# Fused attention and MLP on one core: q and k of batch 2 turned by DMA transposes instead of TensorE

## The chip, the cores and the metric

The kernel runs on one core of a Trainium2 chip. Its engines are TensorE (PE in the profile; PEld is its weight load), VectorE (DVE), ScalarE (ACT), GpSimd (POOL) and SyncE (SP). Each works through its own instructions in order and they wait for each other by semaphores. Sixteen DMA engines move data; here POOL issues the loads, and SP the DMA transposes, the small row copies and the stores of the output. POOL's loads go into one queue (q0 in the profile), SP's into another (q1). The metric is the device time of one execution in microseconds (us), the median over several.

## The reference

Attention with a forgetting decay over 8 batches, 8 heads, 576 tokens, head dimension 64, then a two-layer MLP with the activation h - tanh(h) on all 4,608 tokens:

```python
scores = scale * np.matmul(q, k.transpose(0, 1, 3, 2))
log_f = np.log(np.clip(f, 0.0001, 1.0))
cum = np.cumsum(log_f, axis=-1)
decay = cum[:, :, :, None] - cum[:, :, None, :]
scores = np.where(causal, -1000000000.0, scores + decay)
attn = softmax(scores)                     # written out, with 1e-09 in the divisor
x = (attn @ v).transpose(0, 2, 1, 3).reshape(B * S, H * D)
h = x @ w_in                               # 512 -> 2048
out = (h - np.tanh(h)) @ w_out             # 2048 -> 512
```

## The kernel before

**Slots and pairs.** Attention is done for pairs of heads: 8 batches of 4 pairs, 32 in all. The main loop (L595) runs over slots p = 0 to 32. Slot p emits the scores of pair p in seven tiles (`TILES`, L278; each tile has its matmuls L315, an exp on ACT L324, and from batch 1 on a mask on POOL L334), the values of pair p-1 (matmuls L346, normalised on DVE L353 to L355 into `xn`), and the turn of that pair's output into `XR`, the MLP's input (`turn`, L358: from batch 1 on two DMA transposes on SP, L369 and L371). `att_items` (L537) lists these in order, tile by tile; batch 2 is slots 8 to 11, and slots from 4 on are not "early".

**The MLP in between.** The MLP works on nine units of 512 tokens. A first-layer step (`mlp1`, L387) is four matmuls into one PSUM bank (L397), a tanh on ACT (L402) and a sum on DVE into `gq` (L406). Unit 0's second layer is plain (L432, 16 steps of four matmuls; four steps make one output tile, and the third and fourth of them read the second half of `wout`). Units 1 to 8 use a seven-product scheme with sums and differences of blocks (steps L456; sums of `gq` on DVE, L424, S3 being the first; differences of weights `W1`, `W2`, `W4` and a block of `wout`, L234). `TAKE` says how many MLP steps each slot takes; the loop at L610 spreads them over the slot's items. The banks for the first layer come from a ring (L374): three banks at first, and four, with `ps_tr` added, once `widen(1)` is called in slot 11.

**q and k.** The scores need q and k with the head dimension on the partitions (`QT`, `KT`, two buffers each, by batch parity). There are two ways.
- Batches 0 to 2 (`FAR = 3`): `load_qk` (L89) loads 96 partitions with rows of 768 bytes; in the slot before a pair is used `trans` (L243) turns it on PE (six transposes for q, six for k, L253, into a bank of `ps_tr`), and two copies take it to `QT` or `KT`: for q the first on DVE (L266), the second on ACT (L264) in slots from 4 on, for k both on DVE. k's transposes use the same bank as q's, so they wait for q's second copy.
- Batches 3 to 7: `load_block` (L94) loads five blocks of up to 128 tokens with rows of 128 bytes; `turn_block` (L99) turns each by a DMA transpose on SP (L101) into `TQ` or `TK` (one buffer each); `place` (L103) copies from there into `QT` and `KT`, four copies each, on ACT (L106), DVE or POOL (L108).

**What is emitted where.** `LOADS` maps (slot, tile) to loads, transposes, places and weight differences, and `att_items` emits them there, behind the scores of that tile. Around the change: the halves of `wout` at (4, 0) and (4, 2), q and k of batch 2 at (4, 5) and (4, 6), its v blocks at (5, 0) to (5, 4), the first weight difference at (7, 1). Order on an engine is the order of emission; what is behind a waiting instruction on its engine waits too. POOL's loads share eight semaphores in turn, so that a load is issued only when the eighth load before it has landed.

Of the kernel before, what the change touches and what calls it, by code (L numbers as in the profile page):

```python
# [8 lines left out]
FP32 = mybir.dt.float32  # L9
# [5 lines left out]
PITCH = 640  # L15
VW = 66
SHIFT = 5.0
FAR = 3


@with_exitstack
def kernel(
# [11 lines left out]
    P = 128  # L34
# [48 lines left out]
    vn = [qkp.tile([P, NJ, H, VW], FP16, tag=f"vn{i}", name=f"vn{i}") for i in range(2)]  # L83
    QT = [qkp.tile([D + 3, H, S], FP16, tag=f"QT{i}", name=f"QT{i}") for i in range(2)]
    KT = [qkp.tile([D + 3, H, PITCH], FP16, tag=f"KT{i}", name=f"KT{i}") for i in range(2)]
    TQ = qkp.tile([P, NPAIR, S], FP16, tag="TQ", name="TQ")
    TK = qkp.tile([P, NPAIR, S], FP16, tag="TK", name="TK")

    def load_qk(dst, src, b, h0, h1):  # L89
# [29 lines left out]
        nc.gpsimd.dma_start(out=vn[b % 2][:, n, h0:h1, 0:D],  # L119
                            in_=v[b, h0:h1, n * P:(n + 1) * P, :].rearrange("h p d -> p h d"))  # L120

    lf = TQ[0:NH, :, :].rearrange("p c s -> p (c s)").bitcast(FP32)[:, 0:S]
# [35 lines left out]
    cum = TQ[0:NH, :, :].rearrange("p c s -> p (c s)").bitcast(FP32)[:, S:2 * S]  # L158
# [33 lines left out]
    def load_wout(t0, t1):  # L192
# [7 lines left out]
             (1, 5): [lambda: load_v_rest(1), lambda: load_v_head(1, 0)],  # L200
             (2, 1): [lambda: load_v_head(1, 1), lambda: load_win(DFF // 2, DFF)],
             (4, 0): [lambda: load_wout(0, NFT // 2)],
             (4, 2): [lambda: load_wout(NFT // 2, NFT)]}
    for n in range(NJ - 1):
        LOADS.setdefault((3, n), []).append(lambda n=n: load_v_block(1, n, 2, H))
    LOADS.setdefault((NPAIR, 5), []).append(lambda: load_qk(qn, q, 2, 0, H))
    LOADS.setdefault((NPAIR, 6), []).append(lambda: load_qk(kn, k, 2, 0, H))
    for b in range(2, B):
        p0 = (b - 1) * NPAIR
        for n in range(NJ - 1):  # L210
            LOADS.setdefault((p0 + 1, n), []).append(lambda b=b, n=n: load_v_block(b, n, 0, H))
        LOADS.setdefault((p0 + 1, 4), []).append(lambda b=b: load_v_rest(b))
        LOADS.setdefault((p0, 0), []).append(lambda b=b: load_aug(b))
        if b < FAR:
            continue
        for n in range(NJ):
            qs, ts = ((p0 - 1, n), (p0, 4)) if b == FAR else ((p0 - 2, n + 2), (p0 - 1, 3 if b == FAR + 1 else 1))
            LOADS.setdefault(qs, []).append(lambda b=b, n=n: load_block(qb, q, b, n))
            LOADS.setdefault((p0, n), []).append(lambda b=b, n=n: load_block(kb, k, b, n))
            LOADS.setdefault(ts, []).append(lambda b=b, n=n: turn_block(TQ, qb, b, n))  # L220
            LOADS.setdefault((p0 + 1, 4), []).append(lambda b=b, n=n: turn_block(TK, kb, b, n))
        parts = [(dst, src, a, c) for dst, src in ((QT, TQ), (KT, TK)) for a in range(2) for c in (0, 2)]
        spots = [(p0, 3, "A"), (p0, 5, "A"), (p0 + 1, 0, "A"), (p0 + 1, 2, "A")] + [(p0 + 3, ti, "V") for ti in range(4)]
        if b == FAR:
            spots = [(p0 + 3, ti, eng) for ti, eng in zip((0, 1, 2, 0, 1, 2, 4, 5), "AVAPPPPP")]
        elif b == FAR + 1:
            spots[0:4] = (p0, 5, "A"), (p0, 6, "A"), (p0 + 1, 0, "A"), (p0 + 1, 2, "V")
        for (slot, ti, eng), (dst, src, a, c) in zip(spots, parts):
            LOADS.setdefault((slot, ti), []).append(lambda b=b, dst=dst, src=src, a=a, c=c, eng=eng: place(
                dst, src, b, a, c, eng))  # L230

    def weights(o, x, y, n):
        ks = slice(n * NK // 2, (n + 1) * NK // 2)
        nc.vector.tensor_tensor(out=o[:, ks, :], in0=x[:, ks, :], in1=y[:, ks, :], op=ALU.subtract)  # L234

    SPOTS = [(7, 1), (7, 2), (7, 4), (7, 5), (8, 1), (8, 2), (10, 6), (11, 0)]
    for i, (o, x, y) in enumerate(((W1, B12, B11), (W2, B22, W1), (W4, B21, W2), (B12, B22, B12))):
        for n in range(2):
            LOADS.setdefault(SPOTS[2 * i + n], []).append(lambda o=o, x=x, y=y, n=n: weights(o, x, y, n))
# [3 lines left out]
    def trans(b, c, src, dst, early, copies, split=False):  # L243
        pn, g3 = S // NT6, NT6 // 2
        if early:
            t32 = ps_m.tile([P, UW], FP32, tag="m", name="t32")
            t16 = t32.bitcast(FP16)[:, 0:2 * S // 2].rearrange("p (a g n) -> p a g n", a=2, g=g3)
        else:
            t32 = ps_tr.tile([P, UW], FP32, tag="tr", name="t32")
            t16 = t32.bitcast(FP16)[:, 0:2 * S // 2].rearrange("p (a g n) -> p a g n", a=2, g=g3)  # L250
        for a in range(2):
            for g in range(g3):
                nc.tensor.transpose(out=t16[:, a, g, :],  # L253
                                    in_=src[b % 2][:, 2 * c + a, 2 * g:2 * g + 2, :],
                                    identity=id16[0:pn, 0:pn])
        parts = [(a, e) for a in range(2) for e in range(2)] if split else [(slice(0, 2), e) for e in range(2)]

        def copy(a, e, eng):
            if split:
                a = slice(a, a + 1)  # L260
            to = dst[b % 2][0:D, 2 * c:2 * c + 2, e:S:2].rearrange("d a (p g) -> d a p g", g=g3)[:, a]
            of = t16[e * D:(e + 1) * D, :, :, :].rearrange("d a g p -> d a p g")[:, a]
            if eng == "A":
                nc.scalar.activation(out=to, in_=of, func=AF.Copy)  # L264
            else:
                nc.vector.tensor_copy(out=to, in_=of)  # L266

        todo = [lambda a=a, e=e, eng=eng: copy(a, e, eng) for (a, e), eng in zip(parts, copies)]
        for fn in todo[:2]:
            fn()  # L270
        return todo[2:]

    def head_tiles(a):
        return [[(a, 0, 0, 512, 0)],
                [(a, 1, P, 448, 0), (a, 0, 512, 64, 448)],
                [(a, 2, 2 * P, 320, 0), (a, 3, 3 * P, 192, 320)]]

    TILES = head_tiles(0) + [[(0, 4, 512, 64, 64), (1, 4, 512, 64, 128)]] + head_tiles(1)  # L278
    LAST = 3
# [107 lines left out]
    def mlp1(u, ft, part=None):  # L387
        if part != 1:
            HP[(u, ft)] = bank("hps")
        hps = HP[(u, ft)]  # L390
        t0 = u * UW % RING
        parts = [(0, t0, min(UW, RING - t0))]
        if t0 + UW > RING:
            parts.append((RING - t0, 0, t0 + UW - RING))
        for o, t, n in parts:
            for ci in {None: range(NCH), 0: range(NCH - 1), 1: (NCH - 1,)}[part]:
                nc.tensor.matmul(out=hps[:, o:o + n], lhsT=win[:, ci, ft * P:(ft + 1) * P],  # L397
                                 rhs=XR[:, ci, t:t + n], start=(ci == 0), stop=(ci == NCH - 1))
# [7 lines left out]
        nc.vector.tensor_tensor(out=GQ[(u, i)][:, half, kt, :], in0=hps, in1=th, op=ALU.add)  # L406
        if u >= PLAIN:
            at = (12, 13, 14, 15) if u == 1 else (3, 6, 9, 12)
            if ft in at:
                sums(u, "S3", at.index(ft))  # L410

# [99 lines left out]
    def start():  # L511
        unread(33)
        q_rest = trans(*pairs[0], qn, QT, True, "AAAA", True)
        nc.scalar.activation(out=cq, in_=cum, func=AF.Copy, bias=-SHIFT * inv_qscale, scale=inv_qscale)
        nc.scalar.activation(out=expo, in_=lf[0:1, 0:1], func=AF.Exp)
        unread(6)
        k_rest = trans(*pairs[0], kn, KT, True, "VVVV", True)
        unread(22)
# [18 lines left out]
    def att_items(p):  # L537
# [5 lines left out]
        before = pairs[p - 1] if 0 < p <= len(pairs) else None  # L543
        after = pairs[p + 1] if p + 1 < len(pairs) else None
        early = p < NPAIR
        for ti in range(len(TILES)):
            if here and (p > 0 or ti > 1):
                put(scores, *here, ti)
# [4 lines left out]
                put(unread, 2)  # L553
            if p == 1 and ti == 3:
                put(last)
            for load in LOADS.get((p, ti), ()):
                items.append((load, False))
            at_q, at_k = (1, 3) if p == 0 else (0, 1) if early else (0, 2) if p == NPAIR else (0, 2)
            if ti == at_q and after and after[0] < FAR:
                put(trans, *after, qn, QT, early, "VV" if early else "VA")  # L560
            if p == NPAIR:
                if ti in (3, 4):
                    put(mlp1, 0, ti - 3, 1)
# [84 lines left out]
```

## Time and profile before

| what | us |
|---|---|
| median of 3 runs | 352.4 (352.31 to 352.46) |
| the profiled execution, whole | 352.82 |
| its span in the profile | 351.0 |
| PE busy | 336.5 (96%) |
| DVE, ACT, POOL busy | 259.9, 236.0, 167.6 |
| PE transposes of q and k, L253 (x144) | 10.3 |
| first-layer matmuls, L397 (x640) | 141.4 |

The whole execution is 1.8 us longer than the span of the profile. A matmul's row in the profile ends later than the next one can begin, so time lost on PE is read from start to start. The timeline's column in brackets is the idle time before a group and what ended it. Some rows that matter for the copies (line, engine, operation, out<-in, count; busy us, mean ns of one):

```profile
L266 DVE COPY KT<-t 64x576 f16<-64x576 f16 x22 | 17.6, 800 | 3.8 <-PE t L253 3.6
L106 ACT ACTIVATE QT<-TQ 64x1152 f16<-64x1152 f16 x17 | 19.7, 1158 | 0.2
L264 ACT ACTIVATE QT<-t 64x576 f16<-64x576 f16 x7 | 5.7, 812 | 8.2 <-DVE QT L266 8.2
L108 DVE COPY KT<-TK 64x1152 f16<-64x1152 f16 x16 | 7.4, 460 | 0.2
L108 POOL COPY KT<-TK 64x1152 f16<-64x1152 f16 x4 | 5.3, 1323 | 0.1
```

### The profile page before, as it was taken

The numbers are of one execution on the slowest core, as the hardware profiler recorded it, in microseconds if no ns is written. First come the engines' busy times: TensorE is split into PE (matmuls) and PEld (weight loads), VectorE is DVE, ScalarE is ACT, GpSimd is POOL, SyncE is SP. The second block draws the span as 40 slices with busy tenths as digits, with TensorE's granted clock in tenths as the row PEclk, the third lists the DMA queues.
The fourth block names the chain that finished last, engine by engine and source line by source line (L and its number), as shares of the span: only waits on it lengthen the run. The fifth ranks groups of instructions, "written<-read, shape, count | busy, mean of one in ns | idle before, by whom it ended". The sixth has DMA issues, their size and how long they took to land.

```text
span 351.0 us, 8590 instructions
## 1 busy us (share of the span) xinstructions
PE 336.5 (96%) x3253; PEld 230.7 (66%) x3253; DVE 259.9 (74%) x493; ACT 236.0 (67%) x433; POOL 167.6 (48%) x324
## 2 busy tenths in 40 slices
PE   8998888999889999999999999999999999999996
PEld 7476444555458655875588888855885587477485
DVE  7597577747799588767876787678767866876874
ACT  5587777668695778588868886888648841742640
POOL 8873563776499656575657564752322210000000
PEclk9999999999999999999999999999999999999999
DMA  9999999999978999699969996992031013003003
GB/s 112 144 166 202 192 206 127 112 150 175 113 62 110 152 169 133 77 172 159 114 78 179 151 111 88 174 157 42 23 102 49 18 36 122 0 2 120 0 6 115
DMA packets 144876, 38.79 MB, mean 111 GB/s; under 512 B 128148, under 2 KB 143236, under 8 KB 144836
## 3 DMA queue, kind: packets, MB, share of 16 engines
q0 software_dynamic: 92480, 18.39, 69.7%
q1 hardware_dynamic: 52356, 19.88, 29.7%
q8 instruction: 25, 0.41, 0.5%
q14 instruction: 15, 0.12, 0.1%
HBM read 36.85 MB, written 9.44 MB: 132 GB/s over the span
## 4 chain that ended last, share of the span: by engine, by line
PE 77%; DVE 11%; ACT 7%; issue 2%; DMA 1%; POOL 1%; ACTq 0%; DVEq 0%; POOLq 0%
PE hps L397 28%; PE ops L456 26%; PE ps L315 10%; PE av L346 6%; PE ops L432 3%; ACT e L324 3%; DVE KT L266 3%; DVE gq L406 2%; ACT th L402 2%; DVE QT L266 2%; DVE xn L355 1%; ACT QT L264 1%; PE t L253 1%; DVE gq L424 1%; DMA TQ<-in_f_dram 1%
## 5 line engine op out<-in xcount | busy, mean ns | idle before, releaser
L397 PE MATMUL hps<-XR,win 128*128 128x512 f16 (+1 forms) x640 | 141.4, 357 | 3.1 <-DVE gq L406 1.6
L406 DVE TENSOR_TENSOR gq<-hps,th 128x512 f16<-128x512 f32 x144 | 98.6, 687 | 33.1 <-ACT th L402 31.8
L324 ACT ACTIVATE e<-ps 128x512 f16<-128x512 f32 x192 | 110.0, 598 | 15.5 <-PE ps L315 7.9
L402 ACT ACTIVATE th<-hps 128x512 f32<-128x512 f32 x144 | 86.8, 604 | 49.5 <-PE hps L397 44.3
L334 POOL TENSOR_SCALAR_AFFINE_SELECT e<-e 128x128 f16<-128x128 f16 x168 | 60.6, 363 | 76.7 <-ACT e L324 74.8
L397 PEld LDWEIGHTS <-win 128*128 128x128 f16 x640 | 57.6, 97 | 50.3 <-issue 2.8
L315 PE MATMUL ps<-QT,KT 67*128 67x64 f16 (+5 forms) x384 | 77.2, 276 | 3.1 <-ACT e L324 2.4
L456 PEld LDWEIGHTS <-gq 128*128 128x128 f16 x640 | 60.3, 97 | 12.3 <-DVE gq L424 1.4
L456 PE MATMUL ops<-wout,gq 128*128 128x256 f16 x512 | 63.3, 272 | 1.1 <-DVE gq L424 1.1
L315 PEld LDWEIGHTS <-KT 67*128 67x128 f16 (+1 forms) x384 | 36.9, 98 | 27.9 <-issue 4.8
L346 PEld LDWEIGHTS <-e 128*128 128x128 f16 x896 | 32.1, 97 | 3.1
L346 PE MATMUL av<-vn,e 128*128 128x65 f16 x896 | 33.6, 193 | 0.0
L119 POOL DMA_DIRECT2D vn<-in_v_dram x32 | 28.0, 877 | 10.6 <-DMA win<-in_moe_w_in_dram 4.1
L456 PE MATMUL ops<-W,sq 128*128 128x256 f16 x256 | 31.2, 272 | 0.0
L355 DVE TENSOR_TENSOR xn<-av,rs 128x640 f16<-128x640 f32 x32 | 26.4, 825 | 1.1
L456 PEld LDWEIGHTS <-sq 128*128 128x128 f16 x256 | 24.2, 98 | 3.4
L266 DVE COPY KT<-t 64x576 f16<-64x576 f16 (+1 forms) x26 | 19.5, 750 | 3.8 <-PE t L253 3.6
L334 POOL TENSOR_SCALAR_AFFINE_SELECT el<-el 128x128 f16<-128x128 f16 x28 | 9.5, 338 | 26.8 <-ACT el L324 26.7
L96 POOL DMA_DIRECT2D qn<-in_q_dram x25 | 21.2, 846 | 0.7 <-issue 0.4
L96 POOL DMA_DIRECT2D kn<-in_k_dram x25 | 21.1, 846 | 0.6 <-issue 0.3
L106 ACT ACTIVATE QT<-TQ 64x1152 f16<-64x1152 f16 x17 | 19.7, 1158 | 0.2
L266 DVE COPY QT<-t 64x576 f16<-64x576 f16 x15 | 11.9, 795 | 7.6 <-PE t L253 7.6
(83 smaller groups left out, 301.9 us busy)
## 6 DMA issues: line engine op xcount, KB each, us to landing
out_dram<-ost SPq DMA_DIRECT2D x34, 256.0 KB
vn<-in_v_dram POOLq DMA_DIRECT2D x24, 128.0 KB, 5.6
qn<-in_q_dram POOLq DMA_DIRECT2D x20, 128.0 KB, 4.9
kn<-in_k_dram POOLq DMA_DIRECT2D x20, 128.0 KB, 4.5
win<-in_moe_w_in_dram POOLq DMA_DIRECT2D x2, 1024.0 KB, 14.8
wout<-in_moe_w_out_dram POOLq DMA_DIRECT2D x2, 1024.0 KB, 14.0
XR<-xn SPq DMA_TRANSPOSE x56
vn<-in_v_dram POOLq DMA_DIRECT2D x12, 64.0 KB, 4.8
```

The source lines that it names most:

```text
L96: nc.gpsimd.dma_start(out=dst[b % 2][0:pn, n, :].rearrange("p (h d) -> p h d", h=H), in_=src[b, :, n * P:n * P + pn, :].rearrange("h p d - ...
L119: nc.gpsimd.dma_start(out=vn[b % 2][:, n, h0:h1, 0:D], in_=v[b, h0:h1, n * P:(n + 1) * P, :].rearrange("h p d -> p h d"))
L266: nc.vector.tensor_copy(out=to, in_=of)
L315: nc.tensor.matmul(out=ps[:, col:col + n], lhsT=KT[b % 2][0:rows, h, j * P:(j + 1) * P], rhs=QT[b % 2][0:rows, h, i0:i0 + n], start=not ow ...
L324: nc.scalar.activation(out=e[:, lo:hi], in_=ps[:, lo:hi], func=AF.Exp, scale=qscale)
L334: nc.gpsimd.affine_select(out=view, in_=view, compare_op=ALU.is_ge, fill=0.0, base=0, pattern=pat, channel_multiplier=-1)
L346: nc.tensor.matmul(out=av[:, a, ib, :], lhsT=E.pop((b, c, a, j, ib)), rhs=vn[b % 2][:, j, 2 * c + a, 0:D + 1], start=(j == 0), stop=(j == ib))
L355: nc.vector.tensor_tensor(out=xn.rearrange("p i (a d) -> p a i d", a=2), in0=av[:, :, :, 0:D], in1=rs.to_broadcast([P, 2, NJ, D]), op=ALU. ...
L397: nc.tensor.matmul(out=hps[:, o:o + n], lhsT=win[:, ci, ft * P:(ft + 1) * P], rhs=XR[:, ci, t:t + n], start=(ci == 0), stop=(ci == NCH - 1))
L402: nc.scalar.activation(out=th, in_=hps, func=AF.Tanh, scale=-1.0)
L406: nc.vector.tensor_tensor(out=GQ[(u, i)][:, half, kt, :], in0=hps, in1=th, op=ALU.add)
L456: nc.tensor.matmul(out=ps[:, m, :], lhsT=LHS[lhs](u, kt // 4)[:, kt % 4, m * P:(m + 1) * P], rhs=rhs[:, kt, :], start=(fresh and (apart or ...
```

## The change

`FAR` becomes 2: batch 2 too is loaded in blocks, turned by DMA transposes and placed by copies. `TQ` gets a second buffer. A table by batch says where blocks are loaded, turned and placed; for batch 2 the q blocks are loaded at (4, 1) to (4, 5), the k blocks at (4, 6), (5, 0), (5, 2), (5, 3), (5, 4), the transposes are issued at (5, 1) for q and (6, 0) for k, and the copies stand in slots 7 and 8. The second half of `wout` moves from (4, 2) to (5, 1), behind the q blocks and two k blocks, and batch 2's v blocks from slot 5 to slot 6. All places of q are on ACT and all of k on DVE (batch 3's had been on ACT, DVE and POOL, batch 4's fourth on DVE).

For batch 1 in slots 4 to 6 `trans` now gives only the first copy at once; the second is given one tile later (`rest`), and q's second is on DVE. The ring of four banks starts with slot 7 in place of slot 11, when the last PE transpose is done. The S3 sums of unit 1 stand at steps 3, 6, 9, 12 like those of the other units, and the weight differences get other spots.

```diff
-FAR = 3
+FAR = 2
-    TQ = qkp.tile([P, NPAIR, S], FP16, tag="TQ", name="TQ")
+    TQ = [qkp.tile([P, NPAIR, S], FP16, tag=f"TQ{i}", name=f"TQ{i}") for i in range(2)]
...
-             (4, 2): [lambda: load_wout(NFT // 2, NFT)]}
+             (5, 1): [lambda: load_wout(NFT // 2, NFT)]}
...
-    LOADS.setdefault((NPAIR, 5), []).append(lambda: load_qk(qn, q, 2, 0, H))
-    LOADS.setdefault((NPAIR, 6), []).append(lambda: load_qk(kn, k, 2, 0, H))
+    def add(where, fn, *args):
+        LOADS.setdefault(where, []).append(lambda: fn(*args))
+
     for b in range(2, B):
         p0 = (b - 1) * NPAIR
...
-        if b < FAR:
-            continue
+        at_q = [(p0 - 2, n + 2) for n in range(NJ)]
+        at_k = [(p0, n) for n in range(NJ)]
+        at_v = [(p0 + 1, n) for n in range(NJ)]
+        to_q, to_k = (p0 - 1, 1), (p0 + 1, 4)
+        on_q = (p0, 3), (p0, 5), (p0 + 1, 0), (p0 + 1, 2)
+        on_k = (p0 + 3, 0), (p0 + 3, 2), (p0 + 4, 1), (p0 + 4, 4)
+        if b == 2:
+            at_q = [(p0, n + 1) for n in range(NJ)]
+            at_k = [(p0, 6)] + [(p0 + 1, n) for n in (0, 2, 3, 4)]
+            at_v = [(p0 + 2, n) for n in range(NJ)]
+            to_q, to_k = (p0 + 1, 1), (p0 + 2, 0)
+            on_q = (p0 + 3, 0), (p0 + 3, 2), (p0 + 4, 1), (p0 + 4, 5)
+            on_k = (p0 + 3, 3), (p0 + 3, 5), (p0 + 4, 2), (p0 + 4, 6)
+        elif b == 3:
+            at_q = [(p0 - 1, n) for n in range(NJ)]
+            to_q = p0, 4
+            on_q = (p0 + 3, 1), (p0 + 3, 3), (p0 + 3, 5), (p0 + 4, 1)
+            on_k = (p0 + 3, 2), (p0 + 3, 4), (p0 + 4, 0), (p0 + 4, 4)
+        elif b == 4:
+            on_q = (p0, 6), (p0 + 1, 0), (p0 + 1, 2), (p0 + 1, 4)
+        add((p0, 0), load_aug, b)
...
-        parts = [(dst, src, a, c) for dst, src in ((QT, TQ), (KT, TK)) for a in range(2) for c in (0, 2)]
-        spots = [(p0, 3, "A"), (p0, 5, "A"), (p0 + 1, 0, "A"), (p0 + 1, 2, "A")] + [(p0 + 3, ti, "V") for ti in range(4)]
-        if b == FAR:
-            spots = [(p0 + 3, ti, eng) for ti, eng in zip((0, 1, 2, 0, 1, 2, 4, 5), "AVAPPPPP")]
-        elif b == FAR + 1:
-            spots[0:4] = (p0, 5, "A"), (p0, 6, "A"), (p0 + 1, 0, "A"), (p0 + 1, 2, "V")
...
+            add(at_q[n], load_block, qb, q, b, n)
+            add(at_k[n], load_block, kb, k, b, n)
+            if n < NJ - 1:
+                add(at_v[n], load_v_block, b, n, 0, H)
+            else:
+                add(at_v[n], load_v_rest, b)
+            add(to_q, turn_block, TQ[b % 2], qb, b, n)
+            add(to_k, turn_block, TK, kb, b, n)
+        for n, (c, a) in enumerate(((0, 0), (0, 1), (2, 0), (2, 1))):
+            add(on_q[n], place, QT, TQ[b % 2], b, a, c, "A")
+            add(on_k[n], place, KT, TK, b, a, c, "V")
...
-    SPOTS = [(7, 1), (7, 2), (7, 4), (7, 5), (8, 1), (8, 2), (10, 6), (11, 0)]
+    SPOTS = [(7, 1), (7, 2), (7, 4), (7, 6), (8, 0), (8, 4), (9, 5), (10, 1)]
...
-        for fn in todo[:2]:
+        n = 2 if early else 1
+        for fn in todo[:n]:
             fn()
-        return todo[2:]
+        LATER.extend(todo[n:])
+        return todo[n:]
...
+    LATER = []
+
+    def rest():
+        while LATER:
+            LATER.pop()()
...
-            at = (12, 13, 14, 15) if u == 1 else (3, 6, 9, 12)
+            at = 3, 6, 9, 12
...
+            if p >= NPAIR and ti in (at_q + 1, at_k + 1) and after and after[0] < FAR:
+                items.append((rest, False))
...
-                put(trans, *after, qn, QT, early, "VV" if early else "VA")
+                put(trans, *after, qn, QT, early, "VV")
...
-            if p == 3 * NPAIR - 1:
+            if p == 2 * NPAIR - 1:
                 widen(1)
```

More of the change, by code (lines that the diff above doesn't have):

```diff
@@ L120, in load_v_block @@
                             in_=v[b, h0:h1, n * P:(n + 1) * P, :].rearrange("h p d -> p h d"))
-    lf = TQ[0:NH, :, :].rearrange("p c s -> p (c s)").bitcast(FP32)[:, 0:S]
+    lf = TQ[0][0:NH, :, :].rearrange("p c s -> p (c s)").bitcast(FP32)[:, 0:S]
     nc.sync.dma_start(out=lf, in_=f.rearrange("b h s -> (b h) s"))
@@ L157 @@
     nc.scalar.activation(out=lf, in_=lf, func=AF.Ln)
-    cum = TQ[0:NH, :, :].rearrange("p c s -> p (c s)").bitcast(FP32)[:, S:2 * S]
+    cum = TQ[0][0:NH, :, :].rearrange("p c s -> p (c s)").bitcast(FP32)[:, S:2 * S]
     nc.vector.tensor_tensor_scan(out=cum, data0=ones16, data1=lf, initial=0.0,
@@ L208 @@
     for b in range(2, B):
         p0 = (b - 1) * NPAIR
[L210 to L213, printed above, removed]
-        if b < FAR:
-            continue
-        for n in range(NJ):
[L217 to L221, printed above, removed]
@@ L222 @@
-        parts = [(dst, src, a, c) for dst, src in ((QT, TQ), (KT, TK)) for a in range(2) for c in (0, 2)]
-        spots = [(p0, 3, "A"), (p0, 5, "A"), (p0 + 1, 0, "A"), (p0 + 1, 2, "A")] + [(p0 + 3, ti, "V") for ti in range(4)]
-        if b == FAR:
-            spots = [(p0 + 3, ti, eng) for ti, eng in zip((0, 1, 2, 0, 1, 2, 4, 5), "AVAPPPPP")]
-        elif b == FAR + 1:
-            spots[0:4] = (p0, 5, "A"), (p0, 6, "A"), (p0 + 1, 0, "A"), (p0 + 1, 2, "V")
-        for (slot, ti, eng), (dst, src, a, c) in zip(spots, parts):
-            LOADS.setdefault((slot, ti), []).append(lambda b=b, dst=dst, src=src, a=a, c=c, eng=eng: place(
-                dst, src, b, a, c, eng))
+        at_q = [(p0 - 2, n + 2) for n in range(NJ)]
@@ L517, in start @@
         k_rest = trans(*pairs[0], kn, KT, True, "VVVV", True)
+        LATER.clear()
         unread(22)
@@ L545, in att_items @@
         early = p < NPAIR
+        at_q, at_k = (1, 3) if p == 0 else (0, 1) if early else (0, 2)
         for ti in range(len(TILES)):
@@ L555, in att_items @@
                 put(last)
+            if p >= NPAIR and ti in (at_q + 1, at_k + 1) and after and after[0] < FAR:
+                items.append((rest, False))
             for load in LOADS.get((p, ti), ()):
                 items.append((load, False))
-            at_q, at_k = (1, 3) if p == 0 else (0, 1) if early else (0, 2) if p == NPAIR else (0, 2)
             if ti == at_q and after and after[0] < FAR:
-                put(trans, *after, qn, QT, early, "VV" if early else "VA")
+                put(trans, *after, qn, QT, early, "VV")
             if p == NPAIR:
```

## The prediction, made before the changed kernel had run

> **What bounds the kernel now.** I read first where TensorE (PE) stands still, by stage.
>
> ```profile
> core 0: us, PE busy (x) PEld busy (x) DVE busy (x) ACT busy (x) POOL busy (x), PEclk, DMA share, GB/s
> 38.00:130.00 92.00, 85.66 (x802) 51.59 (x800) 68.36 (x116) 66.73 (x124) 60.12 (x111) 1.00 1.40 141
> 130.00:330.00 200.00, 199.74 (x1893) 141.74 (x1890) 149.66 (x298) 136.47 (x251) 81.11 (x169) 1.00 0.85 94
> ```
>
> From 130 us on PE idles 0.3 us in 200: only less PE work shortens that stretch, and the change takes none away there. From 38 to 130 us (slots 5 to 14; a slot is one pair of heads) PE idles 6.3 us, while the DMA engines are at their busiest. Next, the waits of that stretch (engine and line waited for: total us, times, longest) and their places in PE's order of time:
>
> ```profile
> PE t L253 <- ACT QT L264: 2.3, 3, 0.9
> PE hps L397 <- DVE gq L406: 1.6, 3, 0.6
> PE ops L456 <- DVE gq L424: 1.1, 1, 1.1
> PE ps L315 <- ACT e L324: 1.0, 4, 0.4
> ```
>
> ```profile
> 60.25 0.42 PE L253 MATMUL t<-id,qn 96*128 96x96 f16 x6
> 60.51 1.03 PE L432 MATMUL ops<-wout,gq 128*128 128x512 f16 x4
> ...
> 88.67 0.38 PE L315 MATMUL ps<-QT,KT 67*128 67x320 f16 x2
> 89.71 0.41 PE L253 MATMUL t<-id,kn 96*128 96x96 f16 x6 [0.66 <-ACT QT L264]
> ...
> 93.52 0.38 PE L315 MATMUL ps<-QT,KT 67*128 67x512 f16 x1
> 94.28 1.02 PE L397 MATMUL hps<-XR,win 128*128 128x512 f16 x4 [0.38 <-DVE gq L406]
> 95.14 0.38 PE L315 MATMUL ps<-QT,KT 67*128 67x448 f16 x2
> 96.06 1.02 PE L397 MATMUL hps<-XR,win 128*128 128x512 f16 x4 [0.54 <-DVE gq L406]
> ```
>
> Successive matmuls overlap: four L397 cost 0.86 from start to start (92.66 to 93.52, so 0.22 each), though a row shows 1.03. So a bracketed wait loses 0.16 more than it says: 0.82 at 89.71, 0.54 at 94.28, 0.70 at 96.06. Six transposes cost 0.26 (60.25 to 60.51).
>
> Then the DMAs, one answer per tile: the two halves of the output weights, then batch 2's k, then its v blocks.
>
> ```profile
> L193 POOL DMA_DIRECT2D wout<-in_moe_w_out_dram x2: 881/882/883, 32.2 to 35.1; - x2
> DMA to landing us min/median/max: 12.9/14.0/15.2
> L90 POOL DMA_DIRECT2D kn<-in_k_dram x1: 773/773/773, 40.5 to 40.5; - x1
> DMA to landing us min/median/max: 16.9/16.9/16.9
> L119 POOL DMA_DIRECT2D vn<-in_v_dram x4: 888/892/903, 41.5 to 47.5; - x4
> DMA to landing us min/median/max: 11.4/14.0/16.9
> ```
>
> POOL's queue serves in order and is behind: the halves land at 45.1 (32.2 + 12.9) and 50.3, q (issued 39.3, to landing 13.7) at 53.0, k at 57.4, the five v blocks by 61.3 (the last issued at 49.9, to landing 11.4). So a half costs 5.3 us of queue, q 2.7 as 768 packets of 768 B, k 4.4, five v blocks (4,608 packets of 128 B) 3.9: about 1,200 such packets a us. k took 1.7 longer than q while one pair's 576 transpose packets ran: 2.95 ns each. A second price: from 80 to 86 us 3,042 load packets and 2,357 transpose packets passed; the loads alone need 2.5 us, which leaves 1.5 ns per transpose packet.
>
> **The change, part by part.** Slots start on PE at 38.7, 49.9, 59.8, 67.4, 75.7, 85.6, 97.4 us for slots 5 to 11 (first scores of each pair).
>
> (a) Batch 2's PE transposes go: two groups of six in each of slots 7 to 10, 8 x 0.26 = -2.1. The wait at 89.71 goes with them: -0.8. Their copies go too: 12 DVE copies of 0.80 and four ACT copies of 0.81.
>
> (b) With DVE relieved of 2.4 us per slot and a fourth PSUM bank, the two bank waits (0.54, 0.70) should go: -1.2. Ends: 0 (they move) to -1.2.
>
> (c) The S3 sums of unit 1 move from MLP steps 12 to 15 to steps 3, 6, 9, 12, and the last two weight differences (0.77 each) move about a slot earlier. PE waited for the fourth S3 sum, at 105.32 (1.08 us by the waits; 1.24 from start to start): -1.2, ends 0 and -1.2. DVE was busy 9.9 of the 10 us before 111.
>
> (d) Slots 4 to 6 still transpose batch 1. The second q copy goes from ACT to DVE, and one tile later. ACT's copy started only after DVE's (ACT idles 1.45 <-DVE QT L266 before 53.54), so PE lost 0.92 and 1.03 before the k transposes of slots 5 and 6. After: DVE copies, does one gq (0.69), copies again: 0.80 + 0.61 + 0.80, against 0.80 + 0.83 now, so PE could wait 0.6 more in each. ACT's tanh, no longer behind a copy, runs a us earlier and should end the bank wait in slot 5 (0.64 at 48.20). Ends -1.9 and +1.3; I take +0.3.
>
> (e) The loads. POOL now issues half 1, five q blocks, k blocks 0 and 1, half 2 (slot 5, tile 1), k blocks 2 to 4; the v blocks go to slot 6. No gap opens: each is issued before its turn. Queue work from 45.1: q 3.9, k blocks 0 and 1 1.7, half 2 5.3: 56.0. In between run q's 2,304 transpose packets and one pair's 576: 2,880 x 1.5 to 2.95 ns = 4.3 to 8.5, so half 2 lands between 60.3 and 64.5. I take 1.7 ns (the block-and-block window is the nearer row): 60.9. PE needs it for the third part of the first plain output tile, at 60.51 - 0.26 + 0.3 = 60.6: +0.3, ends 0 and +3.9. POOL's next v block needs the semaphore of half 2, so POOL stops there with three masks of pair 6 behind it; pair 6's values come some 2.5 us later on PE, enough for 0.7 and 3 x 0.35.
>
> (f) The k transposes. SP issues one in 1.3 us (five in 6.54). Behind q's five and one pair's XR, two k blocks go by 58; the others wait for their blocks. Queue work to the last k block: 56.0 + 2.2 = 58.2, plus 2,880 + 1,024 transpose packets, 5.9 to 11.5: between 64.1 and 69.7; at 1.7 ns 64.8. Then 1.25 issue, 1.5 to land (0 to 2.6: the XR issued until 76.8 held up nothing at 79.4), 0.46 for the KT copy on DVE: 68.0. PE's first scores of slot 8 need that copy; PE comes at 67.4 - 0.5 (slot 7's transposes) + 0.3 + 0.3 = 67.5. +0.6, taken as +0.8 since every step must be on time; ends 0 and +6.5. Meanwhile DVE stands at that copy with two weight differences behind it that nobody needs before slot 11; on SP, two XR pairs come up to 5 us later, and unit 1 reads them only at 79.4.
>
> (g) Places. QT copies on ACT rise by 4 x 1.16 (batch 2), 2 x 1.16 (batch 3) and 1.16 (batch 4). In slots 7 and 8 ACT has no tanh, so they hide. In slots 11 to 13 each can hold up an exp, and PE a score: +0.5, ends 0 and +1.5 (four waits of 0.2 to 0.4 there now). KT copies on DVE (0.46) replace POOL copies (1.28): hidden, DVE being 74% busy in the stretch.
>
> [...]
>
> Sum: -2.1 - 0.8 - 1.2 - 1.2 + 0.3 + 0.3 + 0.8 + 0.5 = -3.4. The profiled execution took 352.8 (span 351.0, and 1.8 around it that stays): 349.4. The median of the runs is 0.4 below that execution, so I predict for it 352.4 - 3.4 = **349.0**.
>
> **The rivals.**
> - *The loads are in time, and the copies help*: (e), (f), (g) nothing, (d) -0.5. For it: before 38 us nothing changes, and SP is free when the q blocks land. Against: the queue was behind until 61.3 without 4,608 more transpose packets. 352.4 - 5.3 - 0.5 = 346.6.
> - *The waits only move*: PE is freed, but the next thing in line (exp on ACT, 73% busy from 38 to 130, plus the places) holds it; (b) and (c) bring nothing. For it: four waits on ACT at 116 to 126 stand just behind. Against: after 130 us the same loop runs with four banks and no wait. 352.4 - 2.9 + 1.9 = 351.4.
> - *Slower: the last k block is late, and PE stands before slot 8.* One FIFO holds q, k and half of the weights, transposes take turns with it, and KT hangs on its end. At 2.95 ns per packet half 2 lands at 64.5 (+3.9), and the last k at 69.7: KT at 72.9, against PE at 67.2 + 3.9 = 71.1 (+1.8). 352.4 - 5.3 + 0.8 + 5.7 = 353.6. It decides when the two waits together exceed 4.5. For it: the only row with large packets gives 2.95. Against: the larger row gives 1.5.
>
> **How the numbers follow.** Forecast 0.47 (347.6 to 350.8), loads in time 0.17, waits move 0.17, late k 0.19. Range 346.6 to 353.0: what lies outside is the upper half of the late-k case and a little of the first rival. Below 0.2% (0.7 us) this kernel's runs can't tell a change from none: faster than 351.7 takes the forecast, the first rival and half of the second, 0.72; within, the rest of the second and a little of the last, 0.12; slower 0.16.
>
> **What would show it.** Right: no L253 after 59 us, no bank or S3 wait from 85 to 106; half 2 landing near 61; a stop of PE under 2 us before slot 8's first scores with a DVE KT copy as its end, and the last TK transpose issued near 65. Wrong: L253 waits over 2 us in slots 5 and 6, waits on exp of over 2 us in slots 9 to 13, or KT later than 70 us.

## The result and the profile after

The changed kernel takes 358.49 us (median of 4 runs, 357.74 to 358.91) against 352.4: a ratio of 1.0171 (95% interval 1.015 to 1.0191), 6 us slower. The forecast was 349.0, with a range to 353.0. The profiled execution took 358.1 us, 5.3 more than the one before; its span is 356.0, 5.0 more. The mean granted clock was 0.984 to 0.990 in its four runs, against 1.0 in the profiled execution before.

The place is found as before, by stage (columns: window, its length, busy time and instructions of each engine, granted PE clock, DMA share, GB/s):

```profile
66.00:72.00 6.00, 0.23 (x3) 0.00 (x0) 0.33 (x1) 0.60 (x1) 1.61 (x5) 0.69 1.82 155
72.00:73.00 1.00, 0.82 (x2) 0.28 (x3) 0.97 (x3) 0.12 (x1) 0.00 (x0) 0.50 1.97 151
73.00:78.00 5.00, 5.00 (x33) 2.68 (x32) 2.14 (x4) 3.32 (x5) 2.74 (x5) 0.50 1.56 203
78.00:80.00 2.00, 2.00 (x22) 1.27 (x20) 1.21 (x4) 0.28 (x1) 1.05 (x2) 0.86 1.17 81
80.00:130.00 50.00, 47.96 (x434) 30.43 (x432) 33.33 (x66) 41.08 (x70) 31.57 (x59) 1.00 1.37 136
```

Two things are new. PE does nothing from 66 to 72 us. And from 72 to 78.5 it is busy all the time, but at a granted clock of 0.5: 33 matmuls in five microseconds look like full work in the busy column, and only the clock column tells that they are slow. Before, the clock was 1.00 here. PE's waits from 38 to 130 us, and the order of time around the longest on PE, then on DVE:

```profile
PE ps L336 <- DVE KT L108: 5.9, 1, 5.9
PE t L266 <- DVE QT L279: 2.4, 2, 1.3
PE ps L336 <- ACT e L345: 1.9, 4, 1.0
```

```profile
65.85 0.38 PE L336 MATMUL ps<-QT,KT 67*128 67x320 f16 x2
72.18 0.61 PE L336 MATMUL ps<-QT,KT 67*128 67x512 f16 x1 [5.95 <-DVE KT L108]
72.58 1.91 PE L453 MATMUL ops<-wout,gq 128*128 128x512 f16 x4
```

```profile
61.90 0.82 DVE L376 TENSOR_TENSOR xn<-av,rs 128x640 f16<-128x640 f32 x1
71.67 0.45 DVE L108 COPY KT<-TK 64x1152 f16<-64x1152 f16 x1 [8.94 <-DMA TK<-kn]
```

L336 is the scores' line, L315 before. The bank waits (b) and the S3 wait (c) are no longer in the list. In their place is the first scores of slot 8, which wait for batch 2's KT; DVE's copy had itself waited 8.94 us for the transposes. The same four `wout` matmuls that took 1.03 us a row take 1.91 behind the stop. What the transposes hung on, from the chain that ended last, then the queue of SP:

```profile
45.88 15.81 DMA kn<-in_k_dram
...
63.65 7.89 DMA TK<-kn
```

```profile
44.12 9.51 SPq L101 DMA_TRANSPOSE TQ<-qn  x5
...
56.85 8.96 SPq L101 DMA_TRANSPOSE TK<-kn  x5
```

The k load of the chain landed at 61.69 (45.88 + 15.81) and the last k block at 62.13; the last transpose was issued from 63.65 to 65.8, and its data was there only at 71.54 (63.65 + 7.89). The loads were not late. The second half of `wout` landed at 55.5:

```profile
L193 POOL DMA_DIRECT2D wout<-in_moe_w_out_dram x1: 883/883/883, 43.4 to 43.4; - x1
...
DMA to landing us min/median/max: 12.1/12.1/12.1
```

The whole difference can be followed in the start of each pair's values on PE against before (own reading of the two traces): pair 4 -0.40 us, pair 5 -1.21, pair 6 -2.71; pair 7 +5.72, pair 8 +6.30; then +4.97, +4.74 and, from pair 20 on, +4.95 to +5.10. (At pairs 6 to 9 the changed kernel has done one MLP step of 0.86 us less than the one before, so -2.71 holds 0.86 that is put off and not saved.) Between pairs 6 and 7 the swing is 8.43: the stop, 6.1 from start to start, and half of the 4.66 us from 72.18 to pair 7's values at 76.84, 2.3; two short waits there and the transposes that are gone about cancel. The clock records of the trace put the half clock from 68.31 to 78.55, 10.24 us; PE worked in the last 6.4 of them, so it cost 3.2 in all. Stop and clock together are 9.3; without them the change would have brought 5.3 - 9.3 = -4.0 in this execution (-4.3 by the spans).

### The profile page after: what moved, and what is told of

It reads as the page before. It is cut to its first block, busy times and chain, and to the rows that moved or that the text cites. A ratio compares the mean times of both kernels' runs of the same rounds, so it can differ in the third digit from the quotient of the medians.

```text
span 356.0 us, 8525 instructions
## 1 busy us (share of the span) xinstructions
PE 336.9 (95%) x3205; PEld 230.1 (65%) x3205; DVE 253.3 (71%) x490; ACT 239.6 (67%) x433; POOL 168.7 (47%) x327
## 4 chain that ended last, share of the span: by engine, by line
PE 78%; DMA 10%; ACT 3%; POOL 3%; issue 3%; SPq 1%; DVE 0%; ACTq 0%; POOLq 0%; DVEq 0%
PE hps L418 29%; PE ops L477 25%; PE ps L336 11%; PE av L367 7%; DMA kn<-in_k_dram 4%; DMA wout<-in_moe_w_out_dram 3%; ACT e L345 2%; PE ops L453 2%; DMA TK<-kn 2%; PE idle L526 2%; POOL kn L96 1%; POOL e L355 1%; PE t L266 1%; PE ps L339 1%; PE ps L307 1%
## 5 line engine op out<-in xcount | busy, mean ns | idle before, releaser
L336 PE MATMUL ps<-QT,KT 67*128 67x64 f16 (+5 forms) x384 | 78.6, 278 | 11.5 <-DVE KT L108 5.9
L336 PEld LDWEIGHTS <-KT 67*128 67x128 f16 (+1 forms) x384 | 37.2, 98 | 36.0 <-issue 6.8
L367 PEld LDWEIGHTS <-e 128*128 128x128 f16 x896 | 33.0, 98 | 3.3
L367 PE MATMUL av<-vn,e 128*128 128x65 f16 x896 | 34.4, 194 | 0.0
L106 ACT ACTIVATE QT<-TQ 64x1152 f16<-64x1152 f16 x24 | 27.9, 1162 | 2.3 <-DMA TQ<-qn 1.7
L96 POOL DMA_DIRECT2D qn<-in_q_dram x30 | 25.5, 849 | 2.5 <-issue 2.1
L96 POOL DMA_DIRECT2D kn<-in_k_dram x30 | 25.4, 848 | 1.0 <-issue 0.8
L374 DVE TENSOR_SCALAR rs<-av 128x10 f32<-128x10 f32 x32 | 5.2, 162 | 26.5 <-PE av L367 26.3
L453 PE MATMUL ops<-wout,gq 128*128 128x512 f16 x64 | 18.1, 410 | 0.0
```

Source lines behind the costliest of these rows:

```text
L96: nc.gpsimd.dma_start(out=dst[b % 2][0:pn, n, :].rearrange("p (h d) -> p h d", h=H), in_=src[b, :, n * P:n * P + pn, :].rearrange("h p d - ...
L336: nc.tensor.matmul(out=ps[:, col:col + n], lhsT=KT[b % 2][0:rows, h, j * P:(j + 1) * P], rhs=QT[b % 2][0:rows, h, i0:i0 + n], start=not ow ...
L367: nc.tensor.matmul(out=av[:, a, ib, :], lhsT=E.pop((b, c, a, j, ib)), rhs=vn[b % 2][:, j, 2 * c + a, 0:D + 1], start=(j == 0), stop=(j == ib))
```

## The experiments

Each is measured against the kernel before, run on the same chip beside it. "The changed kernel" is abbreviated C.

**e1_warm: C, with 104 extra matmuls that nobody reads ahead of slot 8's first scores**

```diff
+        if (b, c, ti) == (2, 0, 0):
+            for i in range(104):
+                nc.tensor.matmul(out=ps[:, i % 4 * P:i % 4 * P + P], lhsT=warm, rhs=warm, start=True, stop=True)
```

> The changed kernel with 104 matmuls of 128 columns that nobody reads (about 0.057 us each, 5.9 in all) put on TensorE just before the first scores of slot 8, into the bank that these scores then overwrite. Theory A: after the changed kernel's 6 us stop TensorE's clock was granted at half for 10 us, and that costs about 4 us on top of the stop itself; with the stop filled, the granted clock stays at 1.0 and the time falls from 358.5 to 354.3 (353.8 to 354.9). Rival: the low clock has another cause (power, or chance) and comes again; the time stays within 0.5 of 358.5.

Measured: 356.62 us (354.87 to 357.76), ratio 1.0112 (1.0081 to 1.0144): 1.9 below C where 4.2 was expected. The clock stayed at 1.00:

```profile
66.00:74.00 8.00, 7.86 (x109) 6.41 (x107) 0.00 (x0) 3.08 (x6) 4.89 (x9) 1.00 1.79 148
74.00:80.00 6.00, 5.89 (x68) 3.56 (x65) 5.02 (x10) 3.61 (x6) 3.88 (x6) 1.00 1.65 187
```

In this execution q's transposes too came late (PE stood 2.88 us behind an exp at 65.15, ended by ACT), and KT was copied at 74.33, not 71.67. So slot 8 began 2.66 us later than in C, and yet pair 8's values began 0.39 earlier: the clock was worth 3.0 us, close to the 3.2 above. That keeping PE busy avoids the half clock is shown; the size in the median is blurred by KT's later arrival.

**e2_quiet: C, with batch 2's v in slot 8 and batch 3's loads and transposes one to two slots later**

```diff
-            at_v = [(p0 + 2, n) for n in range(NJ)]
+            at_v = [(8, n) for n in (0, 0, 1, 1, 2)]
...
-            at_q = [(p0 - 1, n) for n in range(NJ)]
-            to_q = p0, 4
+            at_q = [(8, n) for n in (2, 3, 3, 4, 5)]
+            at_k = [(9, n) for n in range(NJ)]
+            at_v = [(10, n) for n in range(NJ)]
+            to_q, to_k = (9, 1), (10, 1)
```

> The changed kernel with batch 2's v blocks moved from slot 6 to slot 8 and batch 3's q blocks from slot 7 to slot 8 (its transposes, k blocks and v blocks follow one to two slots later), so that nothing but batch 2's own loads shares the DMA engines with the k transposes. Theory A: the k transposes land 6 to 8 us after their issue since they take turns with these loads; without them the last lands near 66.5 instead of 71.5, TensorE's stop before slot 8 falls from 6.1 to under 1.5 us, the clock stays at 1.0, and the time falls to about 349.5 (348.5 to 351). Rival B: the last k block stands too late in the queue, behind half of the output weights, and transposes take this long by themselves: the stop stays over 4.5 us and the time over 355.

Measured: 351.95 us (350.56 to 355.65), ratio 0.9993 (0.9952 to 1.0034). On DVE:

```profile
65.64 0.45 DVE L108 COPY KT<-TK 64x1152 f16<-64x1152 f16 x1 [2.94 <-DMA TK<-kn]
```

The last k block landed at 61.69 and the last transpose was issued at 63.17, much as in C; but KT came at 65.64, 6 us earlier, and PE did not wait for it. The lateness was that of the transposes beside other loads. The time fell by 6.5 and not by 9: new stops came, 1.15 at 78.47 for v, now late itself, 1.52 at 102.92 and 1.21 at 122.47 (from start to start, at the start of the matmul ahead; the rows with the waits are at 79.64, 104.52 and 123.76).

**e5_vstays: C, with only the second half of that edit (batch 3 later, batch 2's v back in slot 6)**

> The changed kernel with only batch 3's q, k and v loads and its transposes one to two slots later, as in the earlier run; batch 2's v stays in slot 6. If v alone is what the k transposes take turns with (its blocks landed from 62.97 to 70.73 us, the last k data at 71.54): the stop before slot 8's first scores stays between 4 and 6.5 us, the granted clock falls behind it, and the time is 356 to 358.5. If it is batch 3's q (71.7 to 77.6) that hurts, the stop is under 1 us and the time 351 to 352.5.

Measured: 357.75 us (355.9 to 358.72), ratio 1.0142 (1.011 to 1.0174). DVE, then PE, then ACT:

```profile
72.54 0.45 DVE L108 COPY KT<-TK 64x1152 f16<-64x1152 f16 x1 [9.69 <-DMA TK<-kn]
```

```profile
64.90 0.22 PE L338 MATMUL ps<-QT,KT 67*128 67x64 f16 x2 [2.50 <-ACT e L347]
73.05 0.61 PE L338 MATMUL ps<-QT,KT 67*128 67x512 f16 x1 [2.99 <-DVE KT L108]
```

```profile
63.20 1.16 ACT L106 ACTIVATE QT<-TQ 64x1152 f16<-64x1152 f16 x1 [4.05 <-DMA TQ<-qn]
64.27 1.05 ACT L347 ACTIVATE e<-ps 128x512 f16<-128x512 f32 x2
```

KT is as late as in C with batch 3's loads out of the way, and v is all that this run and e2_quiet differ in: v alone does it (its last block landed at 71.93). The second stop is 2.99 and not 5.95 only because PE had lost 2.50 already behind an exp, which stood on ACT behind a QT copy that waited 4.05 us for q's transposes. In the clock records a stretch at half clock stands at each of the two stops: 3.41 us from 65.15 and 6.83 from 71.97.

**e8_stop: e2_quiet, with the first KT copy of batch 2 written eight more times on DVE**

```diff
+        if b == 2:
+            for _ in range(8):
+                add(on_k[0], place, KT, TK, b, 0, 0, "V")
```

> The kernel with batch 2's v and batch 3's loads moved later, and on DVE the first KT copy of batch 2 written eight more times (0.46 us each), so that PE stands before slot 8's first scores for 3.5 to 4.5 us with no DMA in the way. If a stop of that length alone lowers the clock: granted 0.5 for one or two stretches of 3.4 us behind it, and the time rises by the stop plus 1.5 to 3.4: 356.5 to 359. If the halved clock in the changed kernel came with the DMA traffic: 1.0 throughout, 355 to 356.

Measured: 356.92 us (355.72 to 357.58), ratio 1.0121 (1.0099 to 1.0143). DVE, PE and the windows:

```profile
66.78 4.43 DVE L108 COPY KT<-TK 64x1152 f16<-64x1152 f16 x9 [4.04 <-DMA TK<-kn]
```

```profile
71.27 0.61 PE L341 MATMUL ps<-QT,KT 67*128 67x512 f16 x1 [4.13 <-DVE KT L108]
```

```profile
68.00:70.00 2.00, 0.00 (x0) 0.00 (x0) 1.86 (x5) 0.00 (x0) 0.47 (x1) 1.00 0.40 138
70.00:72.00 2.00, 0.73 (x2) 0.28 (x3) 1.90 (x5) 0.03 (x1) 0.00 (x0) 0.73 0.33 75
72.00:74.00 2.00, 2.00 (x7) 0.81 (x6) 1.97 (x4) 0.95 (x2) 1.36 (x2) 0.50 0.00 0
74.00:76.00 2.00, 2.00 (x35) 1.37 (x33) 0.27 (x1) 1.98 (x4) 2.00 (x4) 0.92 0.84 57
```

PE stood 4.13 us with the transposes already landed, and the clock was halved behind it with a DMA share of 0.00 beside it, while e1_warm had a DMA share of 1.79 at a clock of 1.00: the stop does it, not the traffic. In the clock records the half clock lasts 3.41 us (70.92 to 74.34).

**e3_sums: the kernel before, with only the S3 sums and the weight differences at the change's places**

```diff
-    SPOTS = [(7, 1), (7, 2), (7, 4), (7, 5), (8, 1), (8, 2), (10, 6), (11, 0)]
+    SPOTS = [(7, 1), (7, 2), (7, 4), (7, 6), (8, 0), (8, 4), (9, 5), (10, 1)]
...
-            at = (12, 13, 14, 15) if u == 1 else (3, 6, 9, 12)
+            at = 3, 6, 9, 12
```

> The kernel before with one part of the change alone: the S3 sums of unit 1 at steps 3, 6, 9, 12 and the weight differences at the changed kernel's spots. As predicted for this part: the 1.24 us stop at 105 us goes and nothing else, 351.2 (350.9 to 351.6). Rival: the stop moves on to another wait, 352.2 to 352.6.

Measured: 352.19 us (352.04 to 353.68), ratio 1.0001 (0.9988 to 1.0015). The S3 stop of 1.24 is gone, but the bank wait at 95.07 became 1.17, where it was 0.38 before (the row at 94.28): on DVE a weight difference (0.84) now stands ahead of the two KT copies (1.60) and of the `gq` it waits for. The profiled execution (352.04) is ahead of the one of before by 0.98 at pair 13, and the median by 0.35; the interval of the ratio holds 1, so no gain is shown. Three of the ten runs, at 353.6, have a mean clock of 0.995. With DVE as full as before the sums partly move the wait.

**e4_copies: the kernel before, with only the copies given singly, both q copies on DVE**

```diff
-        for fn in todo[:2]:
+        n = 2 if early else 1
+        for fn in todo[:n]:
             fn()
-        return todo[2:]
+        LATER.extend(todo[n:])
+        return todo[n:]
...
-                put(trans, *after, qn, QT, early, "VV" if early else "VA")
+                put(trans, *after, qn, QT, early, "VV")
```

> The kernel before with one part of the change alone: both q copies of the transposes on DVE, the second copy of q and of k given one tile later, in slots 4 to 10. The trace of the changed kernel shows stops of 1.5 and 1.3 us before the k transposes of slots 5 and 6 (0.9 and 1.0 before), and three other stops of 0.9, 0.8 and 0.3 us between 32 and 49 us gone. If these belong to this part: about 1 us less in slots 4 to 6, and some 0.4 more in each of slots 7 to 10, together 351.5 to 352.8. Rival: the stops that went were not of this part, and it costs: 353.0 or more.

Measured: 353.42 us, ratio 1.0016 (1.0003 to 1.0028), in two groups: 352.25 and 352.31, and five from 353.3 to 353.56. In slots 4 to 6 the copies gain 1.32 us (pair 6), lost again in slot 10, where batch 2's k transposes wait (PE, then windows, of an execution of 353.56):

```profile
89.76 0.43 PE L253 MATMUL t<-id,kn 96*128 96x96 f16 x6 [2.03 <-DVE QT L266]
```

```profile
90.00:92.00 2.00, 2.00 (x31) 1.52 (x29) 1.07 (x2) 0.60 (x1) 0.00 (x0) 0.76 1.12 112
92.00:94.00 2.00, 2.00 (x16) 1.03 (x14) 1.63 (x4) 0.00 (x0) 0.00 (x0) 0.50 0.99 118
```

A stop of 2.03 us was enough for one 3.41 us stretch at half clock (91.03 to 94.44), some 1.7 us of work. The two faster runs have no trace, but their mean granted clocks, 0.997 and 1.0 against 0.992 to 0.995 in the five, agree that they lacked it, and so do their 1.1 us.

**e6_places: e2_quiet, with batch 3's QT copies on POOL and batch 4's as before**

```diff
-            on_q = (p0, 6), (p0 + 1, 0), (p0 + 1, 2), (p0 + 1, 4)
+            on_q = (p0, 5), (p0, 6), (p0 + 1, 0), (p0 + 1, 2)
...
-            add(on_q[n], place, QT, TQ[b % 2], b, a, c, "A")
+            add(on_q[n], place, QT, TQ[b % 2], b, a, c, "P" if b == 3 else "V" if b == 4 and n == 3 else "A")
```

> The kernel with batch 2's v and batch 3's loads moved later, and in it batch 3's four QT copies on POOL and batch 4's four at the spots and engines of the kernel before. If the stops of 1.52 us at 102.92 and 1.21 at 122.47 come from the 1.16 us copies on ACT ahead of an exp: both fall under 0.5, and the time is 1.5 to 2.2 below the 351.38 of that profiled run, 349.2 to 349.9. If the exps are late for another reason (ACT's own load), one stop of about 1 us stays near each place: 350.5 to 351.5.

Measured: 351.83 us (349.78 to 353.71), ratio 0.9981 (0.9957 to 1.0005). The expectation named a wrong cause for one stop. In slot 12 it was not an exp (DVE, then PE):

```profile
106.15 0.45 DVE L108 COPY KT<-TK 64x1152 f16<-64x1152 f16 x1 [5.80 <-DMA TK<-kn]
```

```profile
106.66 0.61 PE L338 MATMUL ps<-QT,KT 67*128 67x512 f16 x1 [2.54 <-DVE KT L108]
```

It is the same wait one batch later: batch 3's transposes beside batch 3's v and batch 4's q (e9_batch3, below, moves these, and the wait goes). In e2_quiet it was 1.36 us by the waits, here 2.54, with a stretch at half clock behind it (0.58 and 0.57 in the windows from 106 to 110). The stop at 122.47, batch 4's, did go. The medians of the two kernels, 351.83 and 351.95, do not differ beyond their spread.

**e7_vsooner and e12_loads: v between the two places**

Both issue batch 2's v in the last three steps of slot 7 and the first two of slot 8. e7_vsooner is e6_places with this edit; e12_loads is e2_quiet with it, with all QT copies on ACT as in the change.

```diff
-            at_v = [(8, n) for n in (0, 0, 1, 1, 2)]
+            at_v = [(7, 4), (7, 5), (7, 6), (8, 0), (8, 1)]
```

> As the run before it, and batch 2's v blocks issued in the last three steps of slot 7 and the first two of slot 8 (they land about 3 us earlier). If the stop of 1.15 us at 78.47 is the fifth v block's landing: it goes, KT stays before 66.5 us since the last TK transpose is issued by 64.4, and the time is 1.1 below that run. If the v packets catch the last TK transposes: KT later by 2 us or more and a stop at slot 8's first scores, with a time at or above that run.

> The changed kernel with loads moved alone: batch 2's v in the last three steps of slot 7 and the first two of slot 8, batch 3's loads and transposes one to two slots later; all QT copies on ACT as in the change. If the 1.16 us copies on ACT cost what their stops say (1.05 to 1.21 us behind an exp, once or twice): 0.8 to 2 above the run with batch 3's copies on POOL, 351.6 to 352.9. If the stops only move (three of those in that run are still there with POOL): within 0.5 of it, 350.4 to 351.4, and the loads alone make the change a gain.

Measured: e7_vsooner 350.86 us (350.12 to 351.45), ratio 0.9952 (0.9933 to 0.9971); e12_loads 351.13 (348.28 to 352.93), ratio 0.9938 (0.9915 to 0.9961). Both beat the kernel before, and C by over 7 us. In the profiled execution of both the stop for v is gone and the clock is 1.00 throughout. They differ by 0.3 in the medians, on two chips and with ranges that overlap, so the QT copies of batches 3 and 4 on ACT cost nothing that shows here, although a stop of 1.05 behind an exp stands in e12_loads at 124.35 and not in e7_vsooner.

**e9_batch3: e7_vsooner, with the same cure for batch 3; e10_onact: that, with batch 3's QT copies on ACT**

```diff
-            at_v = [(10, n) for n in range(NJ)]
+            at_v = [(10, 6)] + [(11, n) for n in range(4)]
...
-            on_q = (p0, 5), (p0, 6), (p0 + 1, 0), (p0 + 1, 2)
+            at_q, to_q = [(11, n + 2) for n in range(NJ)], (12, 2)
+            on_q = (13, 3), (13, 5), (14, 0), (14, 2)
...
-            add(on_q[n], place, QT, TQ[b % 2], b, a, c, "P" if b == 3 else "V" if b == 4 and n == 3 else "A")
+            add(on_q[n], place, QT, TQ[b % 2], b, a, c, "P" if b == 3 else "A")
```

> The run with batch 2's v in slots 7 and 8 and batch 3's QT copies on POOL, and now also batch 3's v loads (slot 10 last step, slot 11) and batch 4's q loads (slot 11, not 10) behind batch 3's k transposes; batch 4's QT copies on ACT at other steps. If the stops of 0.32 to 2.54 us at the first scores of slot 12 (ended by a DVE KT copy that had waited for TK) are the same cause a batch later: KT comes 2 us or more before PE, no such stop, and the time is 349.0 to 350.3, with a narrower spread than 350.12 to 351.45. If they come from elsewhere: a KT wait of over 0.3 stays, 350.3 to 351.3.

> The run before it with batch 3's four QT copies back on ACT as in the changed kernel. If copies of 1.16 us on ACT ahead of an exp hold PE: a stop of about 1 us ended by an ACT exp in slots 11 or 12, and 0.5 to 1.5 more than that run. If they hide: within 0.3 of it.

Measured: e9_batch3 356.72 us (354.27 to 357.9), ratio 1.0098 (1.0073 to 1.0124); e10_onact 357.78 (355.91 to 359.68), ratio 1.0145 (1.0116 to 1.0174). Both are far slower than was expected, though the cause named for slot 12 was right: KT of batch 3 is copied at 101.79 with no wait, and PE's stop at slot 12 is gone. But in e9_batch3 (PE, then POOL):

```profile
110.28 0.27 PE L370 MATMUL av<-vn,e 128*128 128x65 f16 x3 [0.82 <-POOL e L358]
112.61 0.45 PE L370 MATMUL av<-vn,e 128*128 128x65 f16 x9 [2.07 <-POOL e L358]
...
123.79 0.38 PE L421 MATMUL hps<-XR,win 128*128 128x512 f16 x1 [1.35 <-DMA XR<-xn]
```

```profile
110.16 1.14 POOL L108 COPY QT<-TQ 64x1152 f16<-64x1152 f16 x1
111.25 0.88 POOL L96 DMA_DIRECT2D qn<-in_q_dram  x1
112.13 0.42 POOL L358 TENSOR_SCALAR_AFFINE_SELECT e<-e 128x256 f16<-128x256 f16 x1
```

Ten loads from the end of slot 10 through slot 11 keep POOL issuing, 0.69 to 0.89 us each, and its QT copies stand between them, ahead of the masks that the values need; and the q transposes, later by a slot, stand on SP ahead of the XR transposes that the MLP reads. In e10_onact, where POOL has no copies, the mask stops are gone, and the XR wait grew to 3.90 with a half-clock stretch beside it. The stop behind an exp that was expected of copies on ACT is there too, 1.04 at 104.96 after a QT copy of 1.16; with the XR wait and overlapping ranges the 1.06 between the medians does not price it.

**e11_third: e9_batch3, with the k transposes of slots 4 to 6 at step 3**

```diff
-        at_q, at_k = (1, 3) if p == 0 else (0, 1) if early else (0, 2)
+        at_q, at_k = (1, 3) if p == 0 else (0, 1) if early else (0, 3)
```

> The run with batch 3's v later, and in slots 4 to 6 the k transposes of batch 1 a step later (step 3, not 2). If PE's stops of 1.48 and 1.28 us there are the k transposes waiting for the second q copy of DVE to free their bank: both fall under 0.5 and the time is 1 to 2.3 lower, unless the next pair's KT becomes late. If DVE's load as a whole is what holds them, the stop moves to the next reader of DVE and the time is within 0.5.

Measured: 354.77 us (352.5 to 356.91), ratio 1.0063 (1.0038 to 1.0088), 2 below e9_batch3, but that is not where it was meant to come from. The stops before the k transposes went, and pairs 4 and 5 were ahead of the kernel before by 2.27 and 2.66 (0.43 and 1.23 in e9_batch3); by pair 6 it was 2.80 against 2.72, since the next pair's scores now wait for KT:

```profile
48.47 0.39 PE L339 MATMUL ps<-QT,KT 67*128 67x512 f16 x1 [0.95 <-DVE KT L282]
57.86 0.39 PE L339 MATMUL ps<-QT,KT 67*128 67x512 f16 x1 [1.20 <-DVE KT L282]
```

The profiled executions part at pair 7, by 2.7 us, in a stop that varies from one execution to the next: 3.12 at 65.38 with a half-clock stretch behind it in e9_batch3's, 1.18 at 63.37 in e11_third's. Both are behind an exp on ACT that a QT copy held up while it waited for q's transposes. So nothing is claimed for this edit.

## Why the prediction was wrong, by its own steps

- **(f), the k transposes: this step failed.** "Then 1.25 issue, 1.5 to land (0 to 2.6 ...)": the last issue ended at 65.8, near the 66.05 that was forecast (64.8 + 1.25), but the landing took 5.7 us more (7.89 from the start of the issue). The loads came earlier than forecast (last k block 62.1 against 64.8), so the blame that (f) put on k's place in the FIFO was wrong, and so was the condition of the slower rival, that half 2 and the last k block be late: half 2 landed at 55.5, not 64.5.

  What the sum left out is that k's transposes, once issued, were only queued. (f) had 1,024 of k's packets served before the last block landed; by the count of SP's queue (own count, in order of issue) none was: at 62.1 just 2,880 had passed, q's and one pair's XR. k's 2,304 then took 8.6 us (62.1 to 70.7) while 4,263 load packets passed, nearly all of them v's. In e2_quiet, where 102 load packets passed beside them, they took 4.6 (60.4 to 65.1); the 4,263 loads at 1,200 a us are 3.6 more, 8.2 of the 8.6. The prediction had both numbers, 3.9 for v and 1.5 to 2.95 ns for a transpose packet, and added v's nowhere behind the last k block. (Its 1.5 ns counted packets of 4 bytes in; without them 2,994 loads and 2,198 transposes passed from 80 to 86 us, which makes it 1.6.) e2_quiet and e5_vstays differ in v's place alone, and KT comes at 65.64 and 72.54.

  Against the forecast (KT 68.0, PE 67.5) KT came 4.1 us later, at 72.1, and PE 1.4 earlier, at 66.1: with the 0.6 that was forecast, the 6.1 of the stop. So the slower rival had the place and almost the time of KT (72.9), by another cause, and PE waiting there 5 us too late.
- **The halved clock was in no term.** 3.2 us in C by the clock records, 3.0 by e1_warm against C; e8_stop makes it without traffic. Stop and clock are 9.3, where (f) had an end of 6.5. Without the clock's share C would stand near 355.3, still above the range: the stop alone, 6.1 where 0.8 was taken, was enough for that.
- **(a), (b), (c) as forecast.** PE has 3,205 matmuls where it had 3,253, the 48 transposes of (a), and no bank, S3 or k-transpose wait was left from 85 to 106. e3_sums shows why (c) needs (a): in the kernel before, the earlier sums and weight differences made a bank wait grow by 0.79.
- **(d), the copies: wrong sign.** +0.3 was forecast; the copies alone gain 1.32 by pair 6 (e4_copies). The two stops before the k transposes did grow, from 0.92 and 1.03 to 1.48 and 1.28, but first-layer stops of 0.97 (the row at 33.38 in the trace of before), which (d) did not count, and 0.80 (48.20) went: the lower end, -1.9, was the nearer.
- **(e), half 2: nothing lost,** where +0.3 was taken.
- **(g), the QT copies: within its ends, partly at another place.** Stops of 1.04 and 1.05 behind an exp are in C at 112.65 and 130.78, each after a QT copy on ACT, though e7_vsooner and e12_loads differ by only 0.3. "In slots 7 and 8 ACT has no tanh, so they hide" did not hold: batch 2's first QT copy in slot 7 waits for q's transposes with the exps queued behind it. It waited 1.74 us in C, where PE stood 0.18, but 2.20 to 4.67 us in the ten other versions that turn batch 2 by DMA, and PE then stood 0.64 to 3.12 us behind an exp in each. No run moves that copy.
- **Sum.** Without (f) the terms made -4.2, and C's profile without stop and clock -4.0. The versions that avoid both win about 1.5 by their medians, not 4. Their traces show stops that C did not have: in slot 7 that of the QT copy, 1.05 in e7_vsooner and 1.70 in e12_loads, and later 0.96 for XR in e12_loads and waits of 0.3 to 0.6 in e7_vsooner.

What stays open: why runs of e12_loads spread over 4.6 us where those of the kernel before beside them lie within 1.1. The clock is not enough: the run of 351.67 had 1.0, that of 348.28 0.998, and only the slowest, 352.93, shows 0.995. The landings of the transposes differ from run to run (KT of batch 2 was copied at 65.64, 66.74 and 66.78 in three kernels alike up to there, and the stop of batch 2's QT copy is 3.12 in e9_batch3 and 1.02 in e10_onact, which are alike up to there too), which would do it, but no pair of runs isolates it.

## What to carry to other kernels

In C a DMA transpose cost what its queue cost, up to 7.89 us from the start of its issue to its data, not its issue of 2.16: before one is put on the path that sets the end, count the packets that every other queue has in flight until it lands, and put loads that have slack (here v, needed a slot later) behind it. Price a stop of TensorE with the half clock that may come with it (here 3.41 us of it with seven stops of 2.03 to 4.13 us, 10.24 with the 5.95 of C, none with stops of 2.07 and 2.88), and read the clock column before the busy column. Loads that are put off bunch up on the engine that issues them, ahead of what else that engine does: from pair 11 to pair 14 e9_batch3 lost 5.9 us against the kernel before, where e7_vsooner, with its late transposes of batch 3, lost 0.2.

## What the runs showed of the hardware

Stops of PE of 2.03 (e4_copies), 2.50 (e5_vstays), 2.54 (e6_places), 3.12 (e9_batch3), 3.90 (e10_onact) and 4.13 us (e8_stop) each came with one stretch of 3.41 us at half clock, the 2.99 of e5_vstays with 6.83 us and the 5.95 of C with 10.24, two and three times as long. Stops of 1.36 (e2_quiet), 1.70 (e12_loads) and 2.88 (e1_warm) came with none, and the same stop before the values of slot 12 with one in e11_third (2.08) and with none in e9_batch3 (2.07). So the length alone doesn't decide between 2 and 3 us, and what else does is left open. In C's clock records, 68.31 to 78.55 at half clock, the full clock ahead is 61.44 us long and the one behind 276.48, and the half clock began 2.08 us after the end of PE's last row before the stop (66.23).

2,304 packets of DMA transposes took 4.4 to 4.9 us when at most 102 load packets passed beside them (e12_loads, e2_quiet, e8_stop), 1.9 to 2.1 ns each, and 8.6 us in C beside 4,263 load packets of 128 bytes. From the start of its issue to its data a transpose took up to 7.9 us there, where the XR transposes of before held up nothing within 2.6.
